# Batch 1 of a fused attention and SwiGLU kernel: half of its heads transposed by DMA, raw x swapped between partition halves, and one scaled copy made by DVE

## The chip, the cores and the metric

The kernel runs on one core of a Trainium2 chip. The metric is device time in microseconds (us) of one execution; runs of the kernel before and after are taken on the same chip. One execution of each kernel is also recorded by the hardware profiler, and all lines shown from a profile or a trace come from that execution.

The engines are called as the profile calls them: PE multiplies matrices (PEld loads its weights), DVE and ACT work on rows of a tile, POOL and SP issue DMA transfers (SP in hardware queues, POOL in software queues [...]), and 16 DMA engines carry them out.

## The reference

Squared-relu attention over 8 batches of 12 heads, 448 positions and head size 64, and on its result, seen as 3584 tokens of 768 columns, an RMS norm and a SwiGLU block of width 1536:

```python
scores = scale * np.matmul(q, k.transpose(0, 1, 3, 2))
attn = np.maximum(scores, 0.0) ** 2 / S
x = np.matmul(attn, v)                       # [B, H, S, D] -> tokens of H*D
rms = np.sqrt(np.mean(x * x, axis=-1, keepdims=True) + 1e-06)
xn = x / rms * rms_g
g = xn @ w_gate
val = xn @ w_val
out = (g * (1.0 / (1.0 + np.exp(-g))) * val) @ w_out
```

Inputs and output are float32; the kernel loads everything as bf16 and sums in float32.

## The kernel before

**Layout.** Attention is computed transposed: x of a batch is kept as xT, 128 partitions (two heads of 64) by 6 pieces (`kt`) by 448 positions. A second tile, xD, holds the same with the two partition halves swapped, made by `swap` (two DMAs on SP for a range of pieces). Gate and value weights lie in one tile, `wgv_sb`, gate rows in partitions 0 to 63, value rows in 64 to 127; so a round of the gate/value matmuls is a pair, one for gate and one for value, in the two row halves of PE at once, and it needs the pieces of xT for 6 rounds ("own") and those of xD for 6 more.

**Attention of a batch.** q and k must be turned so that the head dimension lies in the partitions. There are two ways. `pe_transposes(b, j)` turns the pair j of heads by 16 PE transposes into a PSUM tile, which DVE or ACT copies to SBUF (line 134, copy at 141 or 143). `transposes(b, half)` turns six heads by two DMA transposes on SP (lines 153 and 157), and `fill` copies two halves of the result across by two more DMAs (lines 165 and 166), so that in the score matmuls positions of a head come in another order, 0, 2, 1, 3 of its four chunks. Scores of one step are two matmuls into a `psS` tile of PSUM (pool `ps_s`, two buffers, shared with the attention-times-V tile `psAV`), then a relu by ACT or DVE to SBUF, and later a square by DVE. `attend` multiplies with V (16 matmuls for two pairs), `leave` lets ACT scale the result into xT and write its square into x2.

**Order.** Nothing is scheduled by a planner. `weave(main, sides)` writes the program order by hand: `main` is a list of units, and each of `sides` has a position ahead of which it stands. Each engine works through its own instructions in that order. The batches are staggered: while the gate/value matmuls of batch b run as main units, the attention steps of batch b+1 are spread between them, and loads and transposes of batch b+2 are issued. `along(p0, gap, fns)` gives positions at equal distance.

Batch 0 is done by `attention_first`, with little else to run beside it. Batch 1 is `attention_second`: all six pairs by `pe_transposes`, steps of one chunk (`pair_scores`), relu on ACT and for the fourth chunk of most pairs on DVE. Batches 2 to 7 are `attention`: both halves by DMA transposes, steps of half a head (`head_scores`).

Four of batch 1's steps stand between the first gate/value blocks of batch 0; the other 31 are spread over the 36 main units of `gate_value(0, EB, KT // 2)` (three rounds each), the last of them, `values(HP - 2)`, being the third V product. On the same list stand the fetch of batch 2 (18.2) and its transposes with fills on POOL (28 and 32).

**Norm.** `norm_stat(b)` sums x2 over partitions by 12 small matmuls (psSS, line 400), takes the root on ACT (with a table load before and one after), the reciprocal on DVE, and spreads it to `rstd`. `norm_apply(b)` multiplies xT with it piece by piece on DVE (line 431), in place except for batch 0. For batch 0 raw xD was made before and is multiplied too; for the others, swaps of the scaled pieces follow each three pieces on SP (line 292).

**Output.** `outproj` makes an output tile of 128 tokens in a piece of 512 and one of 256 columns: 24 matmuls each (line 386), ACT copies from PSUM (line 517), SP stores. The last tile of all is copied half by ACT and half by DVE, and each piece is stored at once (lines 513 to 515). `store` undoes the order 0, 2, 1, 3 of the chunks for the batches that have it. After `gate_value(0)` come three output tiles of batch 0 alone, with batch 1's norm at position 0.

PSUM has besides `ps_s` the pool `ps_m` with four buffers, shared by psT, psG, psV and psO. The transposed tiles kT and qT have two buffers each.

Of the kernel before, what the change touches and what calls it, by code (L numbers as in the profile page):

```python
# [29 lines left out]
def along(p0, gap, fns):  # L30
    return [(p0 + gap * i, f) for i, f in enumerate(fns)]
# [3 lines left out]
def kernel(  # L35
# [52 lines left out]
    def fetch(b):  # L88
        alloc_ld(b)
        for nm in ("q", "k", "v"):  # L90
            load(nm, b)
# [36 lines left out]
    def pe_transposes(b, j):  # L128

        psT = ps_m.tile([P, 2, S], BF16, name="psT", tag="mm")  # L130
        for ti, nm in enumerate(("k", "q")):
            for c in range(NCH):
                for hh in range(2):
                    nc.tensor.transpose(  # L134
                        out=psT[hh * D : (hh + 1) * D, ti, c * PC : (c + 1) * PC],
                        in_=ld[nm, b][:, 2 * j + hh, c * D : (c + 1) * D],
                        identity=ident[:],
                    )
        t = late["qkT"].tile([P, 2, S], BF16, name="qkT", tag="qkT")
        if b and j > 1:  # L140
            nc.scalar.copy(out=t[:], in_=psT[:])
        else:
            nc.vector.tensor_copy(out=t[:], in_=psT[:])
        qkT[b, j] = t
# [95 lines left out]
    def squares(b, j, cs, split=False):  # L240
        r = raw.pop((b, j, cs[0]))
        if split:
            nc.scalar.activation(out=r[:, 0], in_=r[:, 0], func=ACT.Square)
            nc.vector.tensor_tensor(out=r[:, 1], in0=r[:, 1], in1=r[:, 1], op=ALU.mult)
        else:
            nc.vector.tensor_tensor(out=r[:], in0=r[:], in1=r[:], op=ALU.mult)  # L246
        for i, c in enumerate(cs):
            for hh in range(2):
                rsq[b, 2 * j + hh, c] = r[:, i, hh, :]
# [25 lines left out]
    def leave(b, js):  # L275

        psAV = psAVs.pop((b, js))
        for i, j in enumerate(js):
            if b == 0 and j == HP - 1:
                nc.vector.tensor_scalar_mul(  # L280
                    out=xTs[b][:, j, :], in0=psAV[:, i, :], scalar1=ga_sb[:, j : j + 1]
                )
            else:
                nc.scalar.mul(out=xTs[b][:, j, :], in_=psAV[:, i, :], mul=ga_sb[:, j : j + 1])  # L284
        nc.scalar.activation(
            out=x2s[b][:, js[0] : js[-1] + 1, :], in_=psAV, func=ACT.Square, scale=inv_attn
        )
# [37 lines left out]

    def attention_second(b):

        steps = []

        def visit(j, c):  # L330
            pair_scores(b, j, c, c == 3 and j > 0)
            if c == 0 and j:
                squares(b, j - 1, (2, 3))
            if c == 2:
                squares(b, j, (0, 1))

        def values(j):
            attend(b, (j, j + 1))
            leave(b, (j, j + 1))

        for j in range(HP):
            for c in range(NCH):
                steps.append(lambda j=j, c=c: visit(j, c))
                if c == 3 and j + 2 < HP:
                    steps.append(lambda j=j: pe_transposes(b, j + 2))
                if c == 3 and j in (2, 4):
                    steps.append(lambda j=j: values(j - 2))
                    steps.append(lambda: None)
        steps.append(lambda: squares(b, HP - 1, (2, 3)))
        steps.append(lambda: None)  # L350
        steps.append(lambda: values(HP - 2))
        return steps
# [68 lines left out]
    def norm_apply(b):  # L421


        raws = [xTs[b]]
        if b == 0:
            raws.append(xDs[b])
            xTs[b] = npool.tile([P, KT, S], BF16, name="xT", tag="xT", bufs=2)
            xDs[b] = npool.tile([P, KT, S], BF16, name="xD", tag="xD", bufs=2)
        for raw_x, x in zip(raws, (xTs[b], xDs[b])):
            for kt in range(KT):  # L430
                nc.vector.tensor_tensor(  # L431
                    out=x[:, kt, :], in0=raw_x[:, kt, :], in1=rstds[b][:], op=ALU.mult
                )
                if b and kt % 3 == 2:
                    swap(b, kt - 2, kt + 1)

    def hidden(b):
# [61 lines left out]
    osts = {}  # L499

    def outproj(i, t, o, w):
        ps = ps_m.tile([P, 512], FP32, name="psO", tag="mm")
        for fk in range(FT):
            halves(
                ps, w, hTs[i][:, fk, t * P : (t + 1) * P], wo_sb[:, fk, o : o + w],
                fk == 0, fk == FT - 1,
            )
        if o == 0:
            osts[i, t] = late["ost"].tile([P, DM], FP32, name="ost", tag="ost")
        ost = osts[i, t]  # L510
        if (i, t) == (B // 2 - 1, NT - 1):
            mid = o + w // 2
            nc.scalar.copy(out=ost[:, o:mid], in_=ps[:, : w // 2])
            nc.vector.tensor_copy(out=ost[:, mid : o + w], in_=ps[:, w // 2 : w])
            store(i, t, o, o + w, (nc.sync, nc.scalar))
            return
        nc.scalar.copy(out=ost[:, o : o + w], in_=ps[:, :w])  # L517
        if o + w == DM:
            store(i, t, 0, DM, (nc.sync, nc.sync))

    def store(i, t, c0, c1, engs):
        g, end, k = t * P, (t + 1) * P, 0
        while g < end:
            n = min(end, (g // PC + 1) * PC) - g
            b, c, p0 = 2 * i + g // S, g % S // PC, g % PC
            c = c if b < 2 else (0, 2, 1, 3)[c]
            rows = out[b * S : (b + 1) * S, :].rearrange("(p u) m -> p u m", u=NCH)
            engs[k % 2].dma_start(
                out=rows[p0 : p0 + n, c, c0:c1],
                in_=osts[i, t][g - t * P : g - t * P + n, c0:c1],  # L530
            )
            g, k = g + n, k + 1

    def gate_value(b, f0=0, n=KT):
        units = []
        for fb in range(f0, FT):
            for r in range(0, 2 * KT, n):
                units.append(lambda fb=fb, r=r: block_part(b, fb, r, r + n))
        m = KT // n
        units[m : 2 * m], units[2 * m : 3 * m] = units[2 * m : 3 * m], units[m : 2 * m]  # L540
        return units
# [68 lines left out]
    with tc.tile_pool(name="qkT", bufs=2, side="right") as tp, tc.tile_pool(  # L610
        name="early", bufs=EB, side="right"
    ) as ep:
        late["qkT"], late["early"] = tp, ep
        warm(12)
        steps = attention_second(1)
        first = attention_first(0)
        for n, fn in enumerate(first):
            if n == len(first) - 3:
                pe_transposes(1, 0)
            if n == len(first) - 1:  # L620
                pe_transposes(1, 1)
            fn()
            if n % 3 == 2:
                warm(2)
        def early_block(fb):
            return [ps_m.tile([P, S], FP32, name="psE", tag="mm")[:] for _ in range(2)]

        raw_x = xTs[0], xDs[0]
        blocks = [early_block(fb) for fb in range(2)]
        near, far = KT + 4, 2 * KT  # L630
        norm_stat(0)
        rounds(0, 0, blocks[0], 0, KT, raw_x)
        rounds(0, 1, blocks[1], 0, KT, raw_x)
        for fb in range(2):
            steps.pop(0)()
            rounds(0, fb, blocks[fb], KT, near, raw_x)
        norm_apply(0)
        for fb in range(2):
            rounds(0, fb, blocks[fb], near, far, raw_x)
            early_out(0, fb, blocks[fb])  # L640
        for fb in range(2, EB):
            blocks.append(early_block(fb))
            for r0 in range(0, far, KT):
                steps.pop(0)()
                rounds(0, fb, blocks[fb], r0, r0 + KT, raw_x)
            early_out(0, fb, blocks[fb])
        main = gate_value(0, EB, KT // 2)
        sides = along(6.4, 2, [lambda fb=fb: early_scale(0, fb) for fb in range(EB)])
        sides += along(10.4, 2, [lambda fb=fb: early_rest(0, fb) for fb in range(EB)])
        sides += along(0, (len(main) - 1) / len(steps), steps)  # L650
        sides += [(18.2, lambda: fetch(2))]
        sides += [(28, lambda: trans_fill(2, 0)), (32, lambda: trans_fill(2, 1))]
        weave(main, sides)
    late["ost"] = pool("ostage", 3)

# [2 lines left out]
    full = S // P  # L658
    ahead = []
    NB = 2 * FT  # L660
    weave(out_tiles(0, 0, full), [(0, lambda: norm_stat(1)), (0, lambda: norm_apply(1))])
    for b in range(1, B):
        main = gate_value(b)
        if b % 2:
# [46 lines left out]
```

## Time and profile before

| | |
|---|---|
| runs of the kernel before | 457.09, 453.51, 452.74, 456.28, 452.87 us; median 453.51 |
| profiled execution: time | 453.01 us |
| profiled execution: span of the recorded instructions | 451.1 us |
| busy: PE, DVE, ACT, POOL | 439.0, 261.8, 283.0, 53.5 us |
| PE clock granted | full throughout |
| moved by DMA | 53.44 MB, 118 GB/s over the span |

The span counts from the first recorded instruction to the last; the time of an execution also has what lies around it. Busy times are unions: two matmuls that run side by side in two parts of PE count once. In lines of a timeline the first number is the start in us from the start of the span, the second the duration; the bracket at the end says how long the engine was idle before and what ended that. "L451" is line 451 of the kernel before.

The stages in time: attention of batch 0 to about 31 us; first gate/value blocks of batch 0 to 42; the rest of gate/value of batch 0 with batch 1's attention to about 78; three output tiles of batch 0 with batch 1's norm to about 90; from there on gate/value of batch 1 with batch 2's attention, and so on to the last output tiles, from 430.8 us on.

### The profile page before, as it was taken

What the parts mean: (1) busy time and instruction counts of PE and PEld (TensorE: products, weight loads), DVE (VectorE), ACT (ScalarE), POOL (GpSimd) and SP (SyncE); (2) the same over time, 40 slices, a digit from 0 to 9 for tenths busy, and PEclk for the clock granted to TensorE, in tenths of its full rate; (3) what the DMA queues carried; (4) which work ended last, traced back from release to release, by engine and by line L of the source; (5) the groups of instructions that cost most, each with busy time, mean ns of one, the idle gap of its engine ahead of it and who ended that gap; (6) DMA issues with size and microseconds to landing.
All of it is one profiled execution on the core that took longest, in us unless ns stands there. A gap on an engine that the chain in (4) does not pass through costs nothing.

```text
span 451.1 us, 10901 instructions
## 1 busy us (share of the span) xinstructions
PE 439.0 (97%) x4748; PEld 248.1 (55%) x4748; DVE 261.8 (58%) x337; ACT 283.0 (63%) x431; POOL 53.5 (12%) x79
## 2 busy tenths in 40 slices
PE   7999999999999999999999999999999999999996
PEld 3344454755556555655566555655556555665664
DVE  4988975456745666466645666466754466442210
ACT  4888887567765675757655667666757576542221
POOL 8433210400001200030000300003000000000000
PEclk9999999999999999999999999999999999999999
DMA  9999999996008991089905995089913900050013
GB/s 134 197 206 204 200 205 171 206 247 127 0 1 182 196 165 32 22 205 171 140 1 125 189 176 83 2 166 184 155 33 82 212 1 1 1 139 31 1 36 107
DMA packets 86672, 53.44 MB, mean 118 GB/s; under 512 B 36576, under 2 KB 80480, under 8 KB 86624
## 3 DMA queue, kind: packets, MB, share of 16 engines
q0 software_dynamic: 44496, 27.50, 42.2%
q1 hardware_dynamic: 41632, 24.67, 27.3%
q8 instruction: 37, 0.61, 0.5%
q10 hardware_dynamic: 496, 0.57, 0.4%
q14 instruction: 11, 0.09, 0.1%
HBM read 47.19 MB, written 11.01 MB: 129 GB/s over the span
## 4 chain that ended last, share of the span: by engine, by line
PE 86%; ACT 5%; DMA 4%; DVE 3%; issue 1%; SPq 0%; DVEq 0%; ACTq 0%
PE psG L451 37%; PE psO L386 22%; PE psAV L263 8%; PE psV L451 8%; PE psS L218 7%; DMA xD<-xT 3%; ACT r L187 1%; PE psS L177 1%; DMA first_q<-in_q_dram 1%; PE psW L589 1%; PE psT L134 1%; ACT xT L284 1%; PE psSS L400 1%; DVE xT L431 1%; DVE r L246 1%
## 5 line engine op out<-in xcount | busy, mean ns | idle before, releaser
L451 PEld LDWEIGHTS <-wgv_sb 64*128 64x128 bf16 x2304 | 121.2, 94 | 98.0 <-issue 10.5
L451 PE MATMUL psV<-xD,wgv_sb 64*128 64x448 bf16 x558 | 121.6, 349 | 0.5 <-DMA xD<-xT 0.5
L451 PE MATMUL psG<-xT,wgv_sb 64*128 64x448 bf16 x558 | 121.8, 349 | 0.0
L451 PE MATMUL psG<-xD,wgv_sb 64*128 64x448 bf16 x558 | 121.5, 349 | 0.0
L451 PE MATMUL psV<-xT,wgv_sb 64*128 64x448 bf16 x558 | 121.4, 349 | 0.0
L497 DVE TENSOR_TENSOR hT<-sil,psV 128x448 bf16<-128x448 bf16 x93 | 57.6, 619 | 105.7 <-ACT sil L495 101.7
L386 PE MATMUL psO<-wo_sb,hT 128*64 128x512 bf16 (+1 forms) x1344 | 113.5, 326 | 0.0
L232 ACT ACTIVATE r<-psS 112x896 bf16<-112x896 f32 x108 | 96.1, 917 | 22.5 <-PE psS L218 22.4
L386 PEld LDWEIGHTS <-hT 128*64 128x64 bf16 x1344 | 74.8, 110 | 35.2 <-issue 4.1
L495 ACT ACTIVATE sil<-psG 128x448 bf16<-128x448 f32 x93 | 50.7, 545 | 57.4 <-PE psV L451 39.1
L236 DVE TENSOR_TENSOR r<-r 112x1792 bf16<-112x1792 bf16 x72 | 78.4, 1089 | 11.1 <-ACT r L232 10.1
L517 ACT COPY ost<-psO 128x512 f32<-128x512 f32 (+1 forms) x54 | 25.1, 477 | 40.7 <-PE psO L386 34.5
L218 PE MATMUL psS<-qT,kT 64*128 64x448 bf16 (+1 forms) x288 | 47.1, 351 | 0.4 <-DVE r L230 0.4
L284 ACT ACTIVATE xT<-psAV,ga_sb 128x448 bf16<-128x448 f32 x47 | 27.5, 631 | 26.4 <-PE psAV L263 26.4
L230 DVE TENSOR_SCALAR r<-psS 112x896 bf16<-112x896 f32 x36 | 39.1, 1085 | 5.8 <-PE psS L218 5.8
L263 PE MATMUL psAV<-r,vb 112*64 112x448 bf16 x384 | 41.7, 356 | 0.3 <-DVE r L246 0.3
L165 POOL DMA_DIRECT2D qT<-qT x12 | 6.5, 538 | 267.6 <-DMA qT<-qb 199.6
L409 DVE RECIPROCAL rhalf<-rhalf 128x224 f32<-128x224 f32 x8 | 12.4, 1553 | 34.6 <-ACT rhalf L405 34.6
L263 PEld LDWEIGHTS <-vb 112*64 112x64 bf16 x384 | 19.6, 109 | 20.4 <-issue 9.3
L218 PEld LDWEIGHTS <-kT 64*128 64x128 bf16 (+1 forms) x288 | 16.8, 96 | 19.7 <-issue 8.6
L431 DVE TENSOR_TENSOR xT<-xT,rstd 128x448 bf16<-128x448 bf16 x48 | 26.4, 620 | 1.9 <-ACT rstd L418 1.9
L246 DVE TENSOR_TENSOR r<-r 112x1792 bf16<-112x1792 bf16 x23 | 24.5, 1085 | 2.7 <-ACT r L207 2.7
(58 smaller groups left out, 252.0 us busy)
## 6 DMA issues: line engine op xcount, KB each, us to landing
vb<-in_v_dram POOLq DMA_DIRECT2D x7, 672.0 KB, 18.8
xD<-xT SPq DMA_DIRECT2D x28, 168.0 KB, 2.9
qb<-in_q_dram POOLq DMA_DIRECT2D x6, 672.0 KB, 12.5
kb<-in_k_dram POOLq DMA_DIRECT2D x6, 672.0 KB, 15.0
qT<-qT POOLq DMA_DIRECT2D x24, 168.0 KB, 3.6
out_dram<-ost SPq DMA_DIRECT2D x7, 336.0 KB, 6.2
wgv_sb<-in_moe_w_gate_dram POOLq DMA_DIRECT2D x6, 384.0 KB, 16.7
wgv_sb<-in_moe_w_val_dram POOLq DMA_DIRECT2D x6, 384.0 KB, 17.4
```

The lines of the kernel that those rows point to most:

```text
L218: nc.tensor.matmul(out=psS[: end - o, hf, :S], lhsT=flat[prt, o:end], rhs=qT[prt, 1 - hf : 3 - hf, h % HH], start=True, stop=True,)
L230: nc.vector.tensor_relu(out=r[:, cp], in_=src)
L232: nc.scalar.activation(out=r[:, cp], in_=src, func=ACT.Relu)
L236: nc.vector.tensor_tensor(out=r[:], in0=r[:], in1=r[:], op=ALU.mult)
L246: nc.vector.tensor_tensor(out=r[:], in0=r[:], in1=r[:], op=ALU.mult)
L263: nc.tensor.matmul(out=part[hh * D : (hh + 1) * D, :], lhsT=ld["v", b][:, 2 * j + hh, c * D : (c + 1) * D], rhs=rsq[b, 2 * j + hh, c], sta ...
L284: nc.scalar.mul(out=xTs[b][:, j, :], in_=psAV[:, i, :], mul=ga_sb[:, j : j + 1])
L386: nc.tensor.matmul(out=ps[prt, :w], lhsT=lhsT[:, prt], rhs=rhs, start=start, stop=stop)
L431: nc.vector.tensor_tensor(out=x[:, kt, :], in0=raw_x[:, kt, :], in1=rstds[b][:], op=ALU.mult)
L451: nc.tensor.matmul(out=parts[part][:, :S], lhsT=wgv_sb[prt, h, fb * P : (fb + 1) * P], rhs=src[prt, kt, :], start=(r == 0), stop=(r == 2 * ...
L495: nc.scalar.activation(out=s[:], in_=psG, func=ACT.Silu)
L497: nc.vector.tensor_tensor(out=hT[:, fb, o : o + S], in0=s[:], in1=psV, op=ALU.mult)
```

## The change

- Batch 1's heads 0 to 5 stay as they were: PE transposes, steps of one chunk. Heads 6 to 11 are turned by `transposes(1, 1)` with fills on SP, issued ahead of the 36 units, and get steps of half a head with the relu on ACT. `pe_transposes` gives q of batch 1 the chunk order 0, 2, 1, 3, so that both halves of the batch agree, and `store` treats batch 1 as the batches after it.
- Each of batch 1's V products is followed by the swap of the raw pieces that it made. `norm_apply(1)` then multiplies xT and xD by DVE, twelve products in place of six, and issues no swap.
- The third V product of batch 1 leaves the 36 units and stands ahead of the first output piece. The sum of squares, the norm and `trans_fill(2, 1)` (was at 32 of the 36 units) stand one output piece later.
- Since batch 1 has three steps fewer and one of them has left, 27 steps at a distance of 35/28 units take the place of 31 at 35/31.
- The last 256 columns of the last output tile are made as two pieces of 128, each copied by ACT and stored at once; the last tile's 512 piece is copied by ACT alone.

```diff
...
         psT = ps_m.tile([P, 2, S], BF16, name="psT", tag="mm")
         for ti, nm in enumerate(("k", "q")):
             for c in range(NCH):
+                o = (0, 2, 1, 3)[c] if b and ti else c
                 for hh in range(2):
                     nc.tensor.transpose(
-                        out=psT[hh * D : (hh + 1) * D, ti, c * PC : (c + 1) * PC],
+                        out=psT[hh * D : (hh + 1) * D, ti, o * PC : (o + 1) * PC],
                         in_=ld[nm, b][:, 2 * j + hh, c * D : (c + 1) * D],
                         identity=ident[:],
                     )
...
 
     def attention_second(b):
 
+
         steps = []
 
         def visit(j, c):
...
             if c == 2:
                 squares(b, j, (0, 1))
 
+        def visit_head(h, cp):
+            head_scores(b, h, cp, False)
+            if not cp:
+                if h == HH:
+                    squares(b, h // 2 - 1, (2, 3))
+                else:
+                    head_squares(b, h - 1)
+
         def values(j):
             attend(b, (j, j + 1))
             leave(b, (j, j + 1))
-
-        for j in range(HP):
+            swap(b, j, j + 2)
+
+        for j in range(HP // 2):
             for c in range(NCH):
                 steps.append(lambda j=j, c=c: visit(j, c))
-                if c == 3 and j + 2 < HP:
+                if c == 3 and j + 2 < HP // 2:
                     steps.append(lambda j=j: pe_transposes(b, j + 2))
-                if c == 3 and j in (2, 4):
+                if c == 3 and j == 2:
                     steps.append(lambda j=j: values(j - 2))
                     steps.append(lambda: None)
-        steps.append(lambda: squares(b, HP - 1, (2, 3)))
+        for h in range(HH, H):
+            for cp in range(2):
+                steps.append(lambda h=h, cp=cp: visit_head(h, cp))
+                if cp and h == 9:
+                    steps.append(lambda h=h: values(h // 2 - 2))
+                    steps.append(lambda: None)
+        steps.append(lambda: head_squares(b, H - 1))
         steps.append(lambda: None)
         steps.append(lambda: values(HP - 2))
         return steps
...
     def norm_apply(b):
 
 
-        raws = [xTs[b]]
+        raws = [xTs[b]] + ([xDs[b]] if b < 2 else [])
         if b == 0:
-            raws.append(xDs[b])
             xTs[b] = npool.tile([P, KT, S], BF16, name="xT", tag="xT", bufs=2)
             xDs[b] = npool.tile([P, KT, S], BF16, name="xD", tag="xD", bufs=2)
         for raw_x, x in zip(raws, (xTs[b], xDs[b])):
...
                 nc.vector.tensor_tensor(
                     out=x[:, kt, :], in0=raw_x[:, kt, :], in1=rstds[b][:], op=ALU.mult
                 )
-                if b and kt % 3 == 2:
+                if b > 1 and kt % 3 == 2:
                     swap(b, kt - 2, kt + 1)
 
     def hidden(b):
...
     osts = {}
 
     def outproj(i, t, o, w):
+        if (i, t, o) == (B // 2 - 1, NT - 1, 512):
+            for o, w in ((o, w // 2), (o + w // 2, w // 2)):
+                out_piece(i, t, o, w)
+            return
+        out_piece(i, t, o, w)
+
+    def out_piece(i, t, o, w):
         ps = ps_m.tile([P, 512], FP32, name="psO", tag="mm")
         for fk in range(FT):
             halves(
...
             )
         if o == 0:
             osts[i, t] = late["ost"].tile([P, DM], FP32, name="ost", tag="ost")
-        ost = osts[i, t]
+        nc.scalar.copy(out=osts[i, t][:, o : o + w], in_=ps[:, :w])
         if (i, t) == (B // 2 - 1, NT - 1):
-            mid = o + w // 2
-            nc.scalar.copy(out=ost[:, o:mid], in_=ps[:, : w // 2])
-            nc.vector.tensor_copy(out=ost[:, mid : o + w], in_=ps[:, w // 2 : w])
             store(i, t, o, o + w, (nc.sync, nc.scalar))
-            return
-        nc.scalar.copy(out=ost[:, o : o + w], in_=ps[:, :w])
-        if o + w == DM:
+        elif o + w == DM:
             store(i, t, 0, DM, (nc.sync, nc.sync))
 
     def store(i, t, c0, c1, engs):
...
         while g < end:
             n = min(end, (g // PC + 1) * PC) - g
             b, c, p0 = 2 * i + g // S, g % S // PC, g % PC
-            c = c if b < 2 else (0, 2, 1, 3)[c]
+            c = c if b == 0 else (0, 2, 1, 3)[c]
             rows = out[b * S : (b + 1) * S, :].rearrange("(p u) m -> p u m", u=NCH)
             engs[k % 2].dma_start(
                 out=rows[p0 : p0 + n, c, c0:c1],
...
                 rounds(0, fb, blocks[fb], r0, r0 + KT, raw_x)
             early_out(0, fb, blocks[fb])
         main = gate_value(0, EB, KT // 2)
+        transposes(1, 1)
+        fill(1, 1, nc.sync)
         sides = along(6.4, 2, [lambda fb=fb: early_scale(0, fb) for fb in range(EB)])
         sides += along(10.4, 2, [lambda fb=fb: early_rest(0, fb) for fb in range(EB)])
-        sides += along(0, (len(main) - 1) / len(steps), steps)
-        sides += [(18.2, lambda: fetch(2))]
-        sides += [(28, lambda: trans_fill(2, 0)), (32, lambda: trans_fill(2, 1))]
+        sides += along(0, (len(main) - 1) / len(steps), steps[:-1])
+        sides += [(18.2, lambda: fetch(2)), (28, lambda: trans_fill(2, 0))]
         weave(main, sides)
     late["ost"] = pool("ostage", 3)
 
...
     full = S // P
     ahead = []
     NB = 2 * FT
-    weave(out_tiles(0, 0, full), [(0, lambda: norm_stat(1)), (0, lambda: norm_apply(1))])
+    weave(out_tiles(0, 0, full), [(1, lambda: trans_fill(2, 1)), (0, steps[-1]), (1, lambda: norm_stat(1)), (1, lambda: norm_apply(1))])
     for b in range(1, B):
         main = gate_value(b)
         if b % 2:
```

The steps of the program change only here: on PE 48 transposes leave and 24 matmuls come for the last piece's cut, on DVE six products come, three relus and the last tile's two copies leave, on ACT three PSUM copies leave, three relus and one copy of the last tile come, and on SP two transposes, two fills and six raw swaps stand for four swaps of scaled pieces.

## The prediction

> **What bounds the kernel now.** I read the page first (busy shares, the 40 slices), then busy time by stretch, then the timeline of PE alone for its idle gaps, last the timelines of SP and POOL with the DMA view.
>
> ```profile
> PE 439.0 (97%) x4748; PEld 248.1 (55%) x4748; DVE 261.8 (58%) x337; ACT 283.0 (63%) x431; POOL 53.5 (12%) x79
> ...
> PE   7999999999999999999999999999999999999996
> ...
> DMA  9999999996008991089905995089913900050013
> ...
> L451 PE MATMUL psV<-xD,wgv_sb 64*128 64x448 bf16 x558 | 121.6, 349 | 0.5 <-DMA xD<-xT 0.5
> ```
>
> PE is busy 97% of the span at full clock; the only slices below 9 are the first and the last. So an edit pays only where it takes instructions off PE or closes one of PE's few gaps. The 16 DMA engines are full from the start through slice ten, some 113 us: the second thing to watch.
>
> ```profile
> 42.00:78.00 36.00, 34.33 (x385) 18.25 (x384) 26.50 (x32) 28.59 (x43) 5.62 (x7) 1.00 1.36 192
> ...
> 90.00:108.00 18.00, 17.19 (x176) 9.11 (x174) 12.05 (x14) 12.16 (x18) 0.00 (x0) 1.00 1.15 209
> 108.00:430.80 322.80, 322.78 (x3500) 184.52 (x3496) 182.39 (x231) 201.09 (x308) 22.04 (x32) 1.00 0.54 96
> ```
>
> Columns: stretch, busy time and count of PE, PEld, DVE, ACT, POOL, clock, DMA share. From 108 to 430.8 PE is idle 0.02 us of 322.8. The changed stretches, 42 to 78 and 90 to 108, hold 1.67 and 0.81 us of PE idle time, and ACT is 79% and DVE 74% busy in the first. These are the gaps (the bracket: idle time, and what ended it):
>
> ```profile
> 47.72 0.39 PE L134 MATMUL psT<-ident,kb 112*64 112x112 bf16 x8 [0.63 <-ACT sil L495]
> ...
> 59.05 0.37 PE L197 MATMUL psS<-qkT 64*128 64x448 bf16 x2 [0.34 <-ACT r L207]
> ...
> 75.07 0.57 PE L263 MATMUL psAV<-r,vb 112*64 112x448 bf16 x4 [0.34 <-DVE r L246]
> ...
> 77.69 0.38 PE L400 MATMUL psSS<-x,ones_bf 128*64 128x224 bf16 x4 [0.31 <-ACT x L285]
> ...
> 93.73 0.35 PE L451 MATMUL psV<-xD,wgv_sb 64*128 64x448 bf16 x1 [0.45 <-DMA xD<-xT]
> ```
>
> The first is batch 1's transposes of pair 3 waiting for a PSUM buffer; then scores wait for a relu; the last attention-times-V waits for the last square; the sum of squares waits for ACT's square; gate/value waits for the swap of the normalised x. At 92.93 the pair before the last gap started, pairs follow each 0.19 us, so that gap costs 93.73 − 93.12 = 0.61 us rather than the 0.45 shown.
>
> [...] batch 2's first DMA transpose, beside a running fetch, took 9.0 us to land, against 3.6 us for the later one at 103.91. [...] the trace has 6 pieces of 128x448 in 3.30 us, so the six added on xD cost another 3.3. [...] a pair of 256-wide output matmuls takes 1.31/12 = 109 ns, and a pair of 112-wide transposes, loads included, 0.52/8 = 65 ns[...].
>
> **The change part by part.**
>
> *Transposes off PE.* Pairs 3, 4, 5 of batch 1 leave: 48 transposes in three groups, on the chain at 0.58, 0.52 and 0.52 us, 1.6 together. The scores keep their two matmuls a step. The wait of 0.63 ahead of pair 3's group goes with it; next late there is the second gate/value buffer, free at 48.7 when DVE's product at 48.06 is done, and PE gets there at about 48.7. Three PSUM copies of 0.91 leave ACT, three relus of 0.92 come to it from DVE (1.08 each): ACT even, DVE 3.2 lighter. The permuted columns of q and rows of the store change addresses alone.
>
> *ACT in less time.* With 28 steps left for 35 positions the spacing becomes 1.25 units instead of 1.13. In the eight visits of heads 6 to 9 PE has 8 x (1.25 x 0.57 + 0.37) = 8.7 us, while ACT has 8 relus at 0.84 apart, 2.5 Silu at 0.47 and one or two early Silu at 0.52: 8.7 too. Two score buffers then let PE wait now and then. The gap at 59.05 stays, more come: bounds 0 and 1.2 us, I take 0.5.
>
> *Last V product, sum of squares.* The V product now follows the whole gate/value stage, 1.14 us of matmuls later, when the squares are long done: the 0.34 goes. The sum of squares follows 2.6 us of output matmuls, more than ACT's 2.1 for two scalings and the square: the 0.31 goes. The statistic starts later: counted from the end of the V product (t0), ost copy to 3.25, table load to 4.5, root to 5.0, reciprocal and copies to 7.4. xT is done at 10.7, xD at 14.0. PE needs them at t0 + 12.3 and, with two blocks of own halves and scores, about 15: covered by 1 us or more. Batch 2's start at 126.75 to 131.56 already has this order and no gap.
>
> *Swaps of raw x.* The transfer no longer follows the norm, so the 0.61 at 93.73 goes. The six DVE products lie in 9.4 us in which DVE was idle before 94.96. But xT is scaled in place, so DVE must wait for the raw swap to have read it; for the last two pieces that swap is issued after batch 2's transposes on SP.
>
> *DMA.* This is the added cost that the trace doesn't show at its place:
>
> ```profile
> q1 hardware_dynamic: 2752, 0.69, 55.6%
> q0 software_dynamic: 113, 0.21, 17.9%
> ...
> qT<-qb SPq DMA_TRANSPOSE x1, 3.6
> kT<-kb SPq DMA_TRANSPOSE x1, 3.8
> ```
>
> In the 6.5 us from 103.5, two transposes took 55.6% of 16 engines, 3.6 us, and two fills 17.9%, 1.2 us. Together 4.8 us of all engines go in at about 34 us, SP being free after the last raw swap of batch 0; the first two raw swaps of batch 1, 0.23 MB, add some 0.8 (from 84 to 90 the hardware queue's 0.64 MB took 39.7% of 6 us). The engines have no slack there, so what is fetched behind comes about 5.6 us later. Whom this meets:
> - transposes and fills of batch 1 themselves: the fills stand on SP and hold it until the transposes have landed, by about 46, but the next on SP is batch 1's first raw swap at about 54; landed by about 50, scores of head 6 at about 55. Hidden.
> - v of batch 1: landed about 47.3 (an output-weight load waits for it until 47.30). Its first use moves from 54.1 to about 51.8, its landing to 47.3 plus as much as 5: 0 to 1.5 us, I take 0.2.
> - the later gate/value and output weights: 9 us or more early. Hidden.
> - batch 2's q and k:
>
> ```profile
> 69.83 1.37 SPq L153 DMA_TRANSPOSE qT<-qb  x1
> 73.29 3.95 SPq L157 DMA_TRANSPOSE kT<-kb  x1
> 77.28 2.42 SPq L153 DMA_TRANSPOSE qT<-qb  x1
> 79.76 2.96 SPq L157 DMA_TRANSPOSE kT<-kb  x1
> ```
> ```profile
> 79.42 0.54 POOL L165 DMA_DIRECT2D qT<-qT  x1 [21.04 <-DMA qT<-qb]
> 79.95 0.54 POOL L166 DMA_DIRECT2D qT<-qT  x1
> ```
>
> The first transpose was issued when q had landed, at 69.83; the fills at 79.42 waited for it and landed 3.8 us on, about 83. Batch 2's first scores ran at 90.85, 7.9 us later. Now the fills land at about 88.6, a bit earlier since half 1's transposes no longer run beside them, and PE comes at 90.85 less about 2.5 = 88.3. The cover is used up. The last raw swap, behind the k transpose on SP, lands at about 87 and scaled pieces 4 and 5 are then late by some tenths. For both 0 to 3 us; I take 0.4. Half 1 of batch 2 and the fetch of batch 3 on POOL behind its fills move by some 7 us; head 6's scores at about 105 and batch 3's transposes at 103.91, which wait for a kT buffer, cover it.
>
> *The end.*
>
> ```profile
> 446.69 0.27 ACT L513 COPY ost<-psO 128x128 f32<-128x128 f32 x1 [0.91 <-PE psO L386]
> 446.99 0.29 DVE L514 COPY ost<-psO 128x128 f32<-128x128 f32 x1 [0.75 <-ACT ost L513]
> 447.31 0.37 ACTq L528 DMA_DIRECT2D out_dram<-ost  x1
> ```
>
> Two copies follow the last matmul, one behind the other, then the store's issue at 447.31. Now 24 pairs of 128 columns stand for 12 of 256: at 65 ns 1.6 us against 1.3; at 107 (no gain from the narrower piece) 2.6. After the last only one copy of 0.27 is left, but ACT has three copies and three issues to do: 0.59 + 0.38 + 0.27 + 0.37 + 0.27 + 0.37 after the first piece's matmuls, 2.3 us, just the 2.3 from 445.4 to 447.7 now. The last store is half as large. Bounds −0.3 and +0.9; I take +0.1.
>
> **Sum.** Gone: 1.6 + 0.63 + 0.34 + 0.31 + 0.61 = 3.5. New: 0.5 + 0.2 + 0.4 + 0.1 = 1.2. Net −2.3. The profiled execution took 453.01 (span 451.1 and 1.9 around it): 450.7. The median of the runs, 453.51, stands 0.5 above it, so 451.2.
>
> **Rivals.**
> 1. *All covers hold.* ACT keeps up and every transfer is in time: −3.5 and −0.3 at the end, 449.7 by the median. For it: DVE is lighter[...]. Against it: the balance of 8.7 to 8.7 on ACT. A little more than this, by stalls that I don't see, is what faster by over 1% (below 449.0) would need.
> 2. *DMA decides: slower.* The transposes hold the full engines longer than at 103.91, as the 9.0 us of the one at 69.83 hints. If batch 2's q and k come 10 us later instead of 5.6, the fills land at 92.5 to 93, the first scores of batch 2 wait 4.5 and the xT pieces behind the late swap another 1: 451.2 + 5.1 = 456.3. It is slower than before from a delay of about 8 us on; over 1% slower from about 12. Against it: two transposes and fills are 4.8 us of engine time, and PE in order waits only once for the same delay.
> 3. *No net change.* The work taken from PE only uncovers ACT, whose gaps take 1.2 us, and v is late by 1.5, the rest as taken (0.5): 3.2 against 3.5, 453.2. For it: ACT is already the one most often waited for from 55 to 75.
>
> **How the numbers follow.** Forecast 0.58, rival 1 0.20, rival 2 0.12, rival 3 0.10. The forecast's own range is 449.8 to 452.6; with the rivals' times 448.6 to 454.2 leaves out some 2 in 10. One per cent, 4.5 us, is about what a measurement of this kernel can tell from no change: faster by more takes rival 1 and something on top, 0.14; slower by more takes the far end of rival 2, 0.05; within it 0.81.
>
> **What would show it.** Right: PE's waits at L134 for batch 1's later pairs and for xD<-xT at the gate/value line gone, PE's busy time lower by about 1.3 (1.6 off, 0.3 on at the end), idle gaps between 42 and 92 left mostly behind ACT relus. Wrong: a PE gap of over 1 us at the first qT,kT scores of batch 2 or of batch 1, at the first psAV of batch 1 (v late), or at the first psG<-xT of batch 1 after the output tiles; or q of batch 2 landing past 78, which is rival 2.

## The result, and the profile after

The changed kernel takes 457.68 us (median; 453.88 to 460.35, 26 runs) where the kernel before takes 453.47 (452.54 to 458.22, 45 runs): 1.008 of it, with a 95% interval of 1.0065 to 1.010. It is 4.2 us slower. The forecast was 2.3 us faster, with a range up to 454.2; the second rival, *DMA decides*, is what happened. The profiled execution took 457.32 us, its span is 455.5.

The page of the kernel after, the busy shares and three of the 40-slice rows:

```profile
PE 441.4 (97%) x4724; PEld 247.9 (54%) x4724; DVE 261.8 (57%) x338; ACT 283.6 (62%) x432; POOL 53.5 (12%) x79
...
PE   7999999789999999999999999999999999999996
...
PEclk9999999979999999999999999999999999999999
DMA  9999999999405996089903998069912910041013
```

Two slices of PE, the eighth and ninth (80 to 102 us), have fallen below 9, and in the ninth the granted clock has too. PE's busy time was to fall by 1.3 us and rose by 2.4, with 24 matmuls fewer: some of them ran slower. Busy time by stretch, kernel after (columns: stretch, busy time and count of PE, PEld, DVE, ACT, POOL, clock, DMA share, GB/s):

```profile
42.00:78.00 36.00, 35.49 (x371) 19.20 (x367) 24.86 (x31) 29.61 (x45) 5.62 (x7) 1.00 1.34 196
78.00:92.00 14.00, 10.57 (x130) 6.89 (x127) 6.70 (x12) 5.99 (x11) 1.07 (x2) 1.00 1.30 187
90.00:108.00 18.00, 15.54 (x124) 7.82 (x125) 12.49 (x18) 9.36 (x12) 3.89 (x5) 0.81 1.13 203
108.00:430.80 322.80, 322.78 (x3499) 184.24 (x3497) 184.83 (x234) 202.88 (x310) 22.04 (x32) 1.00 0.59 100
```

From 42 to 78, where the change took work and waits away, PE's idle time fell from 1.67 to 0.51 us: that part went as meant. From 78 to 92, where PE was never idle before, it is now idle for 3.43 us. The same stretch in the kernel before:

```profile
78.00:92.00 14.00, 14.00 (x172) 10.00 (x169) 6.02 (x10) 7.44 (x14) 4.96 (x7) 1.00 1.14 208
```

From 90 to 108 the clock is 0.81. From 108 to 430.8 PE is idle for 0.02 us in both kernels. PE's timeline, kernel after, shows the place:

```profile
86.91 0.36 PE L467 MATMUL psG<-xT,wgv_sb 64*128 64x448 bf16 x1
...
87.49 0.35 PE L467 MATMUL psV<-xT,wgv_sb 64*128 64x448 bf16 x1
90.31 0.35 PE L467 MATMUL psG<-xT,wgv_sb 64*128 64x448 bf16 x1 [2.47 <-DVE xT L447]
...
90.84 0.35 PE L467 MATMUL psG<-xT,wgv_sb 64*128 64x448 bf16 x1 [0.17 <-DVE xT L447]
...
92.84 0.95 PE L219 MATMUL psS<-qT,kT 64*128 64x448 bf16 x2 [1.63 <-DMA qT<-qT]
...
94.36 0.57 PE L467 MATMUL psG<-xT,wgv_sb 64*128 64x448 bf16 x1
```

The first gate/value pair of batch 1 starts at 86.91; before, it was at 89.71. So 2.8 us had been won by there, though at the first transposes of 42 us this execution was 0.5 us behind (42.72 against 42.24). Then PE waits 2.47 + 0.17 us for the scaled fifth and sixth pieces of xT and 1.63 us for the fills of batch 2's first q, 4.27 in all. Counted from the 0.19 us at which pairs follow each other, as the prediction did for the gap at 93.73, these waits cost 2.63 + 0.34 + 1.80 = 4.8. The last line shows a 448-column matmul at 0.57 us instead of 0.35: from 92.19 to 99.02 the tensor clock is at half, as the clock column of that stretch says.

```profile
92.19:99.02 6.83, 6.18 (x33) 2.78 (x34) 1.86 (x5) 2.38 (x3) 3.89 (x5) 0.50 0.98 212
```

PE works for 6.18 of these 6.83 us, and pairs follow each 0.37 us instead of 0.19 (93.61, 93.99, 94.36); so half of that, 3.1 us, is lost. The sum is −2.8, −0.6 for the old wait at 93.73 that is gone, +4.8 and +3.1: +4.5. The last batch's output tiles start at 435.27 against 430.85, 4.4 later, and the profiled executions differ by 457.32 − 453.01 = 4.3.

What DVE waited for (its timeline) and what the queues of SP and POOL did (their timelines; "us" is the issue's time, and the transpose is issued when its source has landed):

```profile
89.63 1.16 DVE L447 TENSOR_TENSOR xT<-xT,rstd 128x448 bf16<-128x448 bf16 x2 [5.30 <-DMA xD<-xT]
```

```profile
34.60 1.46 SPq L154 DMA_TRANSPOSE qT<-qb  x1
36.16 7.06 SPq L158 DMA_TRANSPOSE kT<-kb  x1
...
78.25 2.38 SPq L154 DMA_TRANSPOSE qT<-qb  x1
81.73 3.79 SPq L158 DMA_TRANSPOSE kT<-kb  x1
85.62 1.21 SPq L293 DMA_DIRECT2D xD<-xT  x2
```

```profile
87.83 0.54 POOL L166 DMA_DIRECT2D qT<-qT  x1 [22.02 <-DMA qT<-qb]
```

Batch 2's q has landed at 78.25; before it was 69.83. The delay is 8.4 us where 5.6 was worked out. From there it runs down one chain: the k transpose at 81.73 (before 73.29), the last raw swap behind it on SP at 85.62, the fills on POOL at 87.83 (before 79.42), landing when PE's wait ends at 92.84. And the cause of the delay, the DMA view from 38 to 52 us, first of the kernel before and then of the kernel after (columns: packets, MB, time of the packets as a share of 16 engines):

```profile
q0 software_dynamic: 5412, 2.73, 145.3%
```

```profile
q0 software_dynamic: 3069, 1.55, 89.1%
q1 hardware_dynamic: 2812, 0.74, 52.0%
```

In the same 14 us the fetch, q0, moved 1.18 MB less, while q1, nearly all of it the two transposes, moved 0.74. The fetch had run at 2.73 MB / 14 us = 195 GB/s, so it lost 6.0 us. The prediction had charged the transposes 3.6.

### The profile page after: what moved, and what is told of

It is laid out like the page before. It is cut to its first block, busy times and chain, and to the rows that moved or that the text cites. A ratio compares the mean times of both kernels' runs of the same rounds, so it can differ in the third digit from the quotient of the medians.

```text
span 455.5 us, 10870 instructions
## 1 busy us (share of the span) xinstructions
PE 441.4 (97%) x4724; PEld 247.9 (54%) x4724; DVE 261.8 (57%) x338; ACT 283.6 (62%) x432; POOL 53.5 (12%) x79
## 4 chain that ended last, share of the span: by engine, by line
PE 85%; DMA 8%; ACT 3%; issue 1%; DVE 1%; SPq 0%; ACTq 0%; DVEq 0%; POOLq 0%
PE psG L467 35%; PE psO L403 21%; PE psV L467 8%; PE psAV L264 8%; PE psS L219 7%; DMA qb<-in_q_dram 4%; DMA qT<-qb 2%; PE psW L607 2%; ACT r L188 1%; DMA xD<-xT 1%; DMA qT<-qT 1%; PE psS L178 1%; PE psSS L417 1%; PE psE L467 1%; PE psT L135 1%
## 5 line engine op out<-in xcount | busy, mean ns | idle before, releaser
L467 PEld LDWEIGHTS <-wgv_sb 64*128 64x128 bf16 x2304 | 122.9, 95 | 101.8 <-issue 16.0
L233 ACT ACTIVATE r<-psS 112x896 bf16<-112x896 f32 x120 | 106.6, 921 | 29.2 <-PE psS L219 29.0
L403 PE MATMUL psO<-wo_sb,hT 128*64 128x512 bf16 (+2 forms) x1368 | 113.7, 323 | 0.0
L237 DVE TENSOR_TENSOR r<-r 112x1792 bf16<-112x1792 bf16 x78 | 84.9, 1089 | 11.5 <-ACT r L233 10.5
L219 PE MATMUL psS<-qT,kT 64*128 64x448 bf16 (+1 forms) x312 | 53.4, 355 | 2.5 <-DMA qT<-qT 1.6
L533 ACT COPY ost<-psO 128x512 f32<-128x512 f32 (+2 forms) x57 | 26.2, 472 | 42.8 <-PE psO L403 35.8
L219 PEld LDWEIGHTS <-kT 64*128 64x128 bf16 (+1 forms) x312 | 19.2, 97 | 24.4 <-issue 12.4
L286 ACT ACTIVATE x<-psAV 128x896 bf16<-128x896 f32 (+1 forms) x27 | 22.6, 836 | 0.6 <-DVE xT L281 0.6
```

Of the source, the lines that this page charges most:

```text
L219: nc.tensor.matmul(out=psS[: end - o, hf, :S], lhsT=flat[prt, o:end], rhs=qT[prt, 1 - hf : 3 - hf, h % HH], start=True, stop=True,)
L233: nc.scalar.activation(out=r[:, cp], in_=src, func=ACT.Relu)
L403: nc.tensor.matmul(out=ps[prt, :w], lhsT=lhsT[:, prt], rhs=rhs, start=start, stop=stop)
L467: nc.tensor.matmul(out=parts[part][:, :S], lhsT=wgv_sb[prt, h, fb * P : (fb + 1) * P], rhs=src[prt, kt, :], start=(r == 0), stop=(r == 2 * ...
L533: nc.scalar.copy(out=osts[i, t][:, o : o + w], in_=ps[:, :w])
```

## Experiments

Theory A: the DMA transposes of batch 1, put where the engines are full, delay the fetch of batch 2, and this costs the 4.2 us of loss and eats the other parts' gain. Theory B: another part of the change costs the time. Theory C: the order of the issues on SP, with the last raw swap behind batch 2's transposes, costs it, rather than the bytes.

**Heads 6 to 11 by PE transposes again, the rest of the change kept.**

```diff
...
-        for j in range(HP // 2):
+        for j in range(HP):
...
-        transposes(1, 1)
-        fill(1, 1, nc.sync)
...
-            c = c if b == 0 else (0, 2, 1, 3)[c]
+            c = c if b < 2 else (0, 2, 1, 3)[c]
```

> The changed kernel with batch 1's heads 6 to 11 turned by PE again; raw swaps, twelve DVE products, the later V product and sum of squares and the end in pieces of 128 stay. Theory A (the two DMA transposes and fills of batch 1[...] push batch 2's q and k back by 8 us): q of batch 2 lands near 70 again, no PE gap behind DMA between 85 and 95, clock full throughout; against the kernel before only 0.34 + 0.31 + 0.61 = 1.3 us are gained: about 452.2. Theory B (the moved norm, V product and raw swaps themselves cost the time, or ACT and DVE in their new order): stays at 455 or above, with the clock dip.

Measured: 451.43 us (450.79 to 452.16) against 453.73, a ratio of 0.993 [0.990, 0.996]. The later V product and sum of squares, the swaps of raw x, the wider spacing of the steps and the cut last piece are thus a gain of 2.3 us by themselves (1.3 was expected), and this version beats both kernels. Its busy time by stretch and its SP timeline:

```profile
78.00:92.00 14.00, 14.00 (x180) 9.30 (x178) 8.61 (x15) 8.48 (x15) 4.96 (x7) 1.00 1.15 180
```

```profile
70.18 2.60 SPq L154 DMA_TRANSPOSE qT<-qb  x1
74.70 3.48 SPq L158 DMA_TRANSPOSE kT<-kb  x1
78.23 2.67 SPq L293 DMA_DIRECT2D xD<-xT  x2
```

PE is never idle from 78 to 92, q lands at 70.18 (0.35 us later than before), and the last raw swap, still behind the k transpose, is issued 7.4 us earlier than in the kernel after. The order on SP does no harm while q is in time. Theory B fell here.

**The kernel before, plus the same two transposes and fills, which nothing reads.**

```diff
         main = gate_value(0, EB, KT // 2)
+        transposes(1, 1)
+        fill(1, 1, nc.sync)
```

> The kernel before with two DMA transposes and two fills of batch 1's heads 6 to 11 added at the place where the change puts them; nothing reads the result. Theory A: batch 2's q lands at about 78 instead of 69.8, its fills at about 91 to 92; half 1's transposes stand on SP ahead of the swap of the scaled x, which is then issued at about 92 instead of 84; PE waits 5 us or more for xD<-xT and the clock falls to half for some 7 us behind the gap: 460 or more. Theory B: nothing that PE does has changed, 453.5 and at most 1 more.

Measured: 463.19 us (460.38 to 465.84), a ratio of 1.0185 [1.012, 1.025]: some 9 us for four transfers that no instruction uses. The SP timeline, the DMA view from 38 to 52, and PE's timeline of this kernel:

```profile
77.42 2.25 SPq L153 DMA_TRANSPOSE qT<-qb  x1
...
88.53 4.25 SPq L292 DMA_DIRECT2D xD<-xT  x4
```

```profile
q0 software_dynamic: 2958, 1.49, 88.0%
```

```profile
93.95 0.35 PE L451 MATMUL psG<-xD,wgv_sb 64*128 64x448 bf16 x1 [0.62 <-DMA xD<-xT]
...
98.37 0.53 PE L451 MATMUL psG<-xD,wgv_sb 64*128 64x448 bf16 x1 [2.89 <-DMA xD<-xT]
99.65 0.53 PE L451 MATMUL psV<-xD,wgv_sb 64*128 64x448 bf16 x1 [0.75 <-DMA xD<-xT]
```

q of batch 2 lands 7.6 us later than before. The lost fetch explains it: 2.73 − 1.49 = 1.24 MB is 6.3 us, and the two fills would add the 1.2 that the prediction had. The swaps of scaled x, behind batch 2's transposes on SP, are then late, and the clock halves here too, from 96.26 to 103.09. (The profiled execution, 460.38 us, is the fastest of the four.) The two transposes and their fills do it with nothing else of the change.

**The kernel before, plus plain copies of about as many bytes, and the fills.** Three ordinary transfers from the same q and k tiles stand for the two transposes; the third, of 49 KB, fills the last 16 partitions, so they carry 7% more bytes.

```diff
...
+        nc.sync.dma_start(out=flat[:PC, 1344 : 1344 + 1536], in_=ld["q", b][:, hs, :].rearrange("p h m -> p (h m)"))
+        nc.sync.dma_start(out=flat[:PC, 1344 : 1344 + 1536], in_=ld["k", b][:, hs, :].rearrange("p h m -> p (h m)"))
+        nc.sync.dma_start(out=flat[PC:, 1344 : 1344 + 1536], in_=ld["k", b][:16, hs, :].rearrange("p h m -> p (h m)"))
...
         main = gate_value(0, EB, KT // 2)
+        copies(1, 1)
+        fill(1, 1, nc.sync)
```

> As the kernel before with unread transposes, but plain copies in SBUF stand for the two DMA transposes: the same bytes, in rows of some 3 KB instead of packets of 256 B, and the same two fills. Theory A1 (the small packets of the transposes[...] are what costs): the fetch loses about 3 us instead of 8, batch 2's q lands at 72 to 73, a wait of 1 to 2 us for xD<-xT, the time 454 to 456. Theory A2 (the bytes alone): as with the transposes, q at 77 to 78 and 460 or more.

Measured: 459.95 us (458.69 to 460.52), a ratio of 1.014 [1.011, 1.0175]. The DMA view from 38 to 52, and PE's timeline:

```profile
q0 software_dynamic: 4385, 2.21, 118.1%
q1 hardware_dynamic: 348, 0.86, 20.5%
```

```profile
91.40 0.35 PE L228 MATMUL psS<-qT,kT 64*128 64x448 bf16 x1 [0.90 <-DMA qT<-qT]
...
94.08 0.35 PE L461 MATMUL psG<-xD,wgv_sb 64*128 64x448 bf16 x1 [1.01 <-DMA xD<-xT]
96.58 0.35 PE L461 MATMUL psV<-xD,wgv_sb 64*128 64x448 bf16 x1 [2.14 <-DMA xD<-xT]
```

On the fetch the expectation nearly held. In this stretch the hardware queue, with parts of the fills in it, has 348 packets instead of some 2800, and the fetch loses 0.52 MB, 2.6 us, instead of 6.3; q lands at 73.69, 3.9 us late, about the 2.6 and the fills' 1.2. So what the transposes cost the fetch is for the larger part not their bytes. Their 2800 packets of some 260 B may explain it; that the transposing inside them makes a packet slow isn't ruled out, since plain copies in packets of that size weren't tried. On the time the expectation missed: a delay of 3.9 us already makes the scores and the swaps of scaled x late, 4.05 us in the lines above, and the clock halves for 3.4 us. So the plain copies lose 6.5 us, two thirds of what the transposes lose, though they take less than half as much from the fetch: there was less slack behind q than both the prediction and this expectation had.

**The kernel before, plus two unread transposes and two copies late, at 107 to 119 us.**

```diff
...
             sides += [(2, lambda b=b: fetch(b + 2))]
+            if b == 1:
+                sides += [(19, unread)]
```

> The kernel before with the same two unread transposes and two fills, but issued during batch 1's gate/value stage (about 112 us), where the DMA engines are idle. Theory A (full engines make them costly, not the transfers themselves): no PE gap is added, 453.5 within 0.5. If transposes cost PE or SP something wherever they stand: 455 or more.

Measured: 453.51 us (452.09 to 455.69), a ratio of 0.999 [0.996, 1.001], and no gap of PE is added. The same work costs nothing where the engines have room (their share from 107 to 119 us is 0.26 in the kernel before and 0.73 with this work) and 9 us where they have none.

**The last raw swap ahead of batch 2's transposes on SP.**

```diff
-        sides += [(18.2, lambda: fetch(2)), (28, lambda: trans_fill(2, 0))]
+        sides += [(18.2, lambda: fetch(2))]
...
-    weave(out_tiles(0, 0, full), [(1, lambda: trans_fill(2, 1)), (0, steps[-1]), (1, lambda: norm_stat(1)), (1, lambda: norm_apply(1))])
+    weave(out_tiles(0, 0, full), [(1, lambda: trans_fill(2, 1)), (0, steps[-1]), (0, lambda: trans_fill(2, 0)), (1, lambda: norm_stat(1)), (1, lambda: norm_apply(1))])
```

> The changed kernel with batch 2's first two transposes issued behind the last raw swap of batch 1 on SP instead of ahead of it. Theory A: the gap of 2.5 us at xT goes, but the first scores of batch 2 still wait for fills that land at about 92.8: one PE gap of about 4 us in place of two, the clock dip stays, 457 to 458. Theory C (the order on SP, the raw swap behind the transposes, is what costs): the gap and the clock dip go, 452 to 454.

Measured: 456.76 us (453.85 to 460.78), a ratio of 1.006 [1.003, 1.009] over before. PE's timeline and the busy time by stretch:

```profile
55.38 3.20 PE L264 MATMUL psAV<-r,vb 112*64 112x448 bf16 x16 [2.87 <-DMA vb<-in_v_dram]
...
59.98 0.58 PE L467 MATMUL psG<-xT,wgv_sb 64*128 64x448 bf16 x1
```

```profile
94.50 0.35 PE L219 MATMUL psS<-qT,kT 64*128 64x448 bf16 x1 [0.75 <-DMA qT<-qT]
```

```profile
54.56:61.39 6.83, 6.01 (x32) 2.45 (x34) 2.94 (x5) 2.44 (x5) 2.11 (x3) 0.50 1.43 199
...
90.00:108.00 18.00, 16.89 (x180) 9.68 (x178) 13.87 (x20) 11.19 (x16) 4.59 (x7) 1.00 1.14 208
```

The wait for xT is gone and only 0.75 us is left ahead of batch 2's scores, with the full clock from 90 to 108. But this execution doesn't show how much of that the order did, because v of batch 1 came late: its first attention-times-V waited 2.87 us at 55.38, the clock was half from 54.56 to 61.39, and PE reached batch 1's gate/value pairs at 92.21 instead of 86.91, when the transfers had caught up. The medians, 456.76 and 457.68 in the kernel after, differ by 0.9 us, and the intervals of the two ratios overlap. Theory C fell as the main cause: with the order mended the kernel is still slower than before. And the transposes have a second victim, v, whose margin was 4.7 us (landed at 47.3 before, used at 52.0 in the kernel after). In the kernel after's profiled execution v landed at 51.3, just ahead of its use.

**26 dummy matmuls ahead of batch 1's gate/value stage**, so that PE isn't idle in the gap.

```diff
+    warm(26)
     for b in range(1, B):
         main = gate_value(b)
```

> The changed kernel with 26 dummy matmuls of 448 columns (about 4.9 us) ahead of batch 1's gate/value matmuls, where PE would otherwise wait. If the idle gap is what halves the clock for 6.8 us (3.4 us lost), PE stays at full clock and the time falls by about 2.5 to 3, to about 455, although PE has 4.9 us more to do. If the clock falls for another reason, it stays at 457.5 or rises.

Measured: 458.86 us (456.19 to 459.92), a ratio of 1.008 [1.003, 1.012] over before, against 455 expected: a miss. PE's timeline:

```profile
55.21 1.70 PE L264 MATMUL psAV<-r,vb 112*64 112x448 bf16 x16 [3.18 <-DMA vb<-in_v_dram]
...
90.10 5.09 PE L607 MATMUL psW<-warm_in 128*128 128x448 bf16 x26
...
97.44 0.35 PE L219 MATMUL psS<-qT,kT 64*128 64x448 bf16 x1 [0.82 <-DMA qT<-qT]
```

The clock stayed full in the whole profiled execution, and the seven executions have mean clocks of 0.995 to 1.0, where 25 of the 26 of the kernel after have 0.987 to 0.996. This fits the gap's lack of work as what lowers it. But the dummy work took 5.09 us in PE's order, more than the waits for xT that it stood for, and v was late by 3.18 us on top. What the clock costs can't be read from this run.

**The last raw swap first, and v of batch 2 fetched behind batch 2's fills.** On POOL's queue, v's load stands between k's and the fills in the kernel after, and shares the engines with the transposes.

```diff
-        sides += [(18.2, lambda: fetch(2)), (28, lambda: trans_fill(2, 0))]
+        sides += [(18.2, lambda: (alloc_ld(2), load("q", 2), load("k", 2)))]
...
-    weave(out_tiles(0, 0, full), [(1, lambda: trans_fill(2, 1)), (0, steps[-1]), (1, lambda: norm_stat(1)), (1, lambda: norm_apply(1))])
+    weave(out_tiles(0, 0, full), [(1, lambda: trans_fill(2, 1)), (0, steps[-1]), (0, lambda: (trans_fill(2, 0), load("v", 2))), (1, lambda: norm_stat(1)), (1, lambda: norm_apply(1))])
```

> The changed kernel with the last raw swap ahead of batch 2's transposes on SP, and batch 2's v fetched behind their fills instead of ahead of them, so that these transposes run beside less traffic. Theory A: q and k still land near 78 and 81, but the transposes then take about 4 us instead of 9, the fills land at about 87 to 88, PE's wait there falls below 1 us. What is left is a late v of batch 1 in part of the executions (up to 3 us and a half-clock stretch): 452 to 455, ahead of the changed kernel by 3 or more. Theory B: unchanged at 456 to 458.

Measured: 453.66 us (450.99 to 455.55), a ratio of 0.9985 [0.996, 1.001]: the same as before, and 4 us better than the kernel after. The timelines of SP, POOL and PE:

```profile
77.36 1.75 SPq L154 DMA_TRANSPOSE qT<-qb  x1
```

```profile
83.47 0.55 POOL L166 DMA_DIRECT2D qT<-qT  x1 [19.35 <-DMA qT<-qb]
```

```profile
89.55 0.35 PE L219 MATMUL psS<-qT,kT 64*128 64x448 bf16 x1 [1.15 <-DMA qT<-qT]
```

q's transpose is still 7.5 us later than before, but the fills are issued 4.4 us earlier than in the kernel after. PE reaches batch 1's first pair at 86.91, as there, doesn't wait for xT, and 1.15 us of wait are left at the scores (below 1 was expected). So the loss follows when the fills and the last raw swap are done: q's delay, and what the queues put behind it. Still, with both orders mended the DMA transposes bring nothing over PE's, which need 451.4.

## Why the prediction was wrong

- *Transposes off PE*, *Last V product, sum of squares*, *ACT in less time*: right. The waits at L134, for the last square and for the sum of squares are gone. Of the gaps behind ACT only 0.31 us at 59.56 and 0.17 at 69.26 are left, 0.48 where 0.5 was taken. Batch 1's first gate/value pair came 2.8 us earlier, 3.3 counted from 42 us, where the steps gave 1.6 + 0.63 + 0.34 + 0.31 − 0.5 − 0.2 = 2.2; v's 0.2 didn't fall due in this execution, and 0.9 isn't placed. In the first experiment, without the first of these steps, the same pair came 1.33 earlier (88.38) where the two waits are 0.65. Part of this is that brackets put waits too low, as the prediction saw at 93.73; the rest isn't shown.
- *Swaps of raw x*: the wait for xD went (the first experiment shows it), as long as q of batch 2 is in time. The prediction had named the dependence, "DVE must wait for the raw swap to have read it", and the swap's place behind batch 2's transposes; it charged "some tenths", and 2.64 us came.
- *DMA*: the step that failed, in two terms. First, the transposes' price. The figure "two transposes took 55.6% of 16 engines, 3.6 us" was read at 103.5, where they ran almost alone, and applied at 36 to 52, where they ran beside the fetch. The sum was worked in engine time. Counting packets gives the measured size: before, the fetch sent 5412 packets of some 504 B in 14 us; after, 3069 of them beside 2812 of the transposes, of some 260 B. The fetch sent 2343 fewer, nearly one packet for one packet, at half the bytes: 6.0 us instead of 3.6, the packets' own share of time having grown from 55.6% of 6.5 us to 52.0% of 14 us, 7.3 us. (That the engines share themselves out by packets is an estimate from these counts; it isn't shown otherwise.) With the prediction's 1.2 for the fills and 0.8 for the raw swaps that is 8.0, and 8.4 was measured.
- The second term is the weight. The prediction had found that at a delay of 5.6 us "The cover is used up", gave 0 to 3 us, and took 0.4. With no slack left each further microsecond is paid: 2.8 us more on q made 1.63 at the scores and 2.64 at the xT pieces, 4.27 where 0.4 was taken. The plain copies show that even 3.9 us of delay was too much for the kernel before. The claim against rival 2, that "PE in order waits only once for the same delay", failed: the late swap and the late fills made two waits one after the other, since the fills landed at 92.84, 2.0 us after PE got the last scaled pieces at 90.84, with 0.2 us of work between.
- v of batch 1, "0 to 1.5 us, I take 0.2": 0 in the kernel after's profile, but 2.87 and 3.18 in two others with the same transposes. The upper bound came from the too low delay.
- Batch 1's own transposes, called hidden with their fills landed "by about 50": q's landed at 47.4, the fills at about 54.5, and the scores of head 6 started at 54.79. They came just in time; the 5 us of cover were used up here too.
- What no step had is the clock. After these waits it ran at half for 6.83 us, which is 3.1 us on top of them. The runs of the kernel after fit this: the one with a mean clock of 1.0 took 453.88, level with before; those at 0.996 took 456.1 to 458.2, those at 0.987 took 459.0 to 460.4. So in that one execution the waits ate the gain and no more, and by and large the loss is greater where the clock was lower. How much of a run's spread is the clock itself and how much the longer waits that come with it isn't separated.
- *The end*: +0.1 taken. From the last output tiles' start to the end of the span it is 20.19 us, and was 20.24; right. ACT's timeline, kernel after, shows the three copies and issues behind one another, with a second issue that took 0.79:

```profile
450.87 0.27 ACT L533 COPY ost<-psO 128x128 f32<-128x128 f32 x1 [0.45 <-PE psO L403]
451.16 0.79 ACTq L546 DMA_DIRECT2D out_dram<-ost  x1
451.99 0.27 ACT L533 COPY ost<-psO 128x128 f32<-128x128 f32 x1 [0.86 <-ACT ost L533]
```

Rival 2 had the chain right: "batch 2's q and k come 10 us later", fills at 92.5 to 93 (measured 92.84 landed), and 456.3 us. That its number is near is partly luck: it had a longer delay than the 8.4 measured, 5.5 us of waits where 4.3 to 4.8 came, and no clock, which took 3.1. It had 0.12 because the delay was priced at 5.6; with 8.0, by packets, it would have deserved more.

One reading was off without weight: in the row of the page the tenth slice of DMA is 6, so the engines are full through the ninth, some 101 us, and not to 113.

## What to carry to other kernels

Moving work from the bound engine to full DMA engines wasn't free here: with the DMA transposes the kernel takes 457.68 us, with PE's 451.43. Count the packets that run beside the fetch (here 2812 of the transposes for 2343 fewer of the fetch), and not only the bytes or the transfer's time when alone, and follow the delay to the first transfer with the least slack. Where the sum uses that slack up to nothing, forecast the wait instead of a fraction of it, and add the price of a lower clock: in four executions here PE was idle for 1.9 to 2.7 of 3.4 us, and then half clock followed for 3.4 or 6.8 us. At a place where the engines had room (a share of 0.26 from 107 to 119 us), the same transfers cost nothing (a ratio of 0.999).

## What the runs showed of the hardware

- The tensor clock fell with PE not wholly idle. In the kernel after it is full from 6.86 to 92.19, half to 99.02 and full to 454.00: 85.33, 6.83 and 354.98 us, or 25, 2 and 104 times 3.413. Half clock lasted 6.83 us too with the last raw swap first and with the unread transposes, and 3.41 with the plain copies. In the 3.41 us just ahead of the fall PE was busy for 0.73 us in the kernel after, 1.09 with the plain copies, 1.37 with the last raw swap first and 1.55 with the unread transposes. This stretch of the kernel after:

```profile
88.78:92.19 3.41, 0.73 (x4) 0.26 (x4) 2.56 (x5) 0.00 (x0) 0.12 (x1) 1.00 1.08 204
```

The length of a single wait doesn't decide: half clock came after one of 2.87 us (the last raw swap first), and not after one of 3.18 us (the dummy matmuls, from 52.03 to 55.21). Nor does the work in the 3.41 us just ahead: up to 55.21 that was 0.2 us, and the clock stayed full. Divided at 54.02 instead, the time around this wait holds more work in each part:

```profile
50.61:54.02 3.41, 1.42 (x15) 0.59 (x13) 3.41 (x5) 1.79 (x3) 0.00 (x0) 1.00 1.30 220
54.02:57.44 3.42, 2.23 (x24) 1.15 (x26) 2.69 (x4) 0.49 (x1) 0.95 (x2) 1.00 1.60 190
```

So where such a stretch begins may matter; this is an estimate, from the whole multiples above and from this one wait. What brings the clock down is not shown. Stretches of 3.41 us with 0.73 to 1.55 us of work were followed by half clock, stretches with 1.42 (above) and 1.67 (plain copies, from 90.55) were not: near 1.5 us PE's busy time alone doesn't decide.

- A DMA transpose of 344 KB was some 1400 small packets (2752 for two at 103.5). Beside a running fetch two of them kept 1.18 to 1.24 MB away from it, plain copies of 7% more bytes, in some 350 packets with parts of their fills, 0.52 MB. The engines together sent 5432 packets from 38 to 52 us in the kernel before and 5884 in the kernel after, but 2.77 and 2.32 MB: the number of packets stayed much the same, and the bytes fell.
